# Linear attention and a gated feed-forward on one core: scores as pairs of 64-row tiles, weight loads as jobs of the order, two normalisations on GpSimd

## The chip, the core and the metric

The kernel runs on one core of a Trainium2 chip. A core has a matrix engine (TensorE, "PE" in the profile, its weight loads "PEld"), a vector engine (VectorE, "DVE"), a scalar engine (ScalarE, "ACT"), GpSimd ("POOL"), which computes and also issues the loads from memory, and SyncE ("SP"), which issues stores and transposing transfers. Each engine works through its own list of instructions in order and waits on semaphores for the others. Matrix results land in PSUM, eight banks of 128 partitions by 512 fp32. The metric is the device time of one launch in microseconds, as the median of several runs.

## What is computed

```python
k_proj = np.einsum('ks,bhsd->bhkd', E, k)          # 8 batches, 8 heads, 1024 x 64 -> 64 x 64
v_proj = np.einsum('ks,bhsd->bhkd', F, v)
scores = (1/8) * np.matmul(q, k_proj.transpose(0, 1, 3, 2))
scores = scores - np.max(scores, axis=-1, keepdims=True)
attn = np.exp(scores)
attn = attn / (np.sum(attn, axis=-1, keepdims=True) + 1e-09)
x = np.matmul(attn, v_proj)                        # -> (8192 tokens, 512)
gate = 1.0 / (1.0 + np.exp(-(x @ w_gate)))         # 512 -> 1536
val = x @ w_val
out = (gate * val) @ w_out                         # 1536 -> 512
```

All inputs are fp32; they are turned to bf16 on loading.

## The kernel before

Eight batches of 1024 tokens go through attention one after another, and each batch's tokens go through the feed-forward part as two blocks of 512. The feed-forward products are mostly made with seven instead of eight partial products (Winograd's form of Strassen's scheme): `quad_jobs` and `o_jobs` write them, with sums of weights (`w_sum`, `o_sum`), of inputs (`xs_sum`) and of hidden values (`s_sum`) made on VectorE and GpSimd. The first block is made plainly, by `plain_steps`.

A load puts eight consecutive tokens of a head on one partition, so a 128-column piece of Q holds two groups of tokens (g = 0, 1), 64 features each. After transposing, `qT[:, h, t * P : (t + 1) * P]` has on its 128 rows the 64 features of group 0 and the 64 of group 1, for token tile t (four tiles a batch) and head h. The projected keys stand in `kpD[:, h, :]` as a block diagonal: rows 0 to 63 and columns 0 to 63 for group 0, the rest for group 1, and zeros elsewhere. `score` (L1615) makes a score with one full 128x128 weight load and one matmul of 128 columns per head, four heads to a bank; half of what is multiplied is zero. So a token tile has two visits of TensorE (y = 0, 1), each into one bank. Behind it `highest` (L1633) takes the maximum on VectorE, `lower` (L1647) subtracts it (on VectorE for the later batches), `exps` (L1671) takes the exponential on ScalarE into `pt`, and `turn_p` sends the tile through a transposing transfer to `eT`.

Three kinds of TensorE jobs use a part of the array: the K and V projections (`project0`, `project_v0`, `kv`, `apart`: two tiles of 128 rows by 64 columns) and the first batch's output (`h_xo`: four tiles of 64 by 64, in two banks). All others use the full array.

The first batch has its own path in halves (`first_batch`, L784): projections as the halves of K and V land, scores, `total0` and `norm0` (sum, reciprocal, normalisation; L976, L983), transposes on TensorE, outputs. There `ORDER` also holds negative numbers, which `busy` (L720) turns into fillers: matmuls of the identity, -2 for 512 columns and -1 for 256, that keep TensorE going while it would wait.

Nothing is scheduled at run time. Each step is registered as a job in the order of the code; `ORDER` (L159) lists the job numbers in the order in which they are put on their engines, and `PLACES` (L314) lists the PSUM bank or SBUF buffer of each. The positions, costs and landing times (`AT`, `FB`, `K_AT`, `LAND`) given to `job` do nothing in this program: `Scheduler.job` drops them.

All loads go through GpSimd's queue. `start_loads` (L614) issues 25 of them ahead of every job: halves of K and Q, V, then the gate and value weights in column blocks j = 0 to 5, G (gate) and V (value), the first in halves (h0, h1).

Of the kernel before, what the change touches and what calls it, by code (L numbers as in the profile page):

```python
# [40 lines left out]
    f_pv00=0, f_pv01=0, f_pv10=1, f_pv11=1, f_s00=1, f_s01=1, f_s10=0, f_s11=0, f_n00=0, f_n01=0, f_n10=1,  # L41
# [3 lines left out]
    f_dk=0, f_w2=1, f_late=0, f_q1=0, f_q2=0, f_wsG0=1, f_wsG1=0, f_wsG2=0, f_wsV0=1, f_wsV1=0, f_wsV2=0,  # L45
    f_xs0=0, f_xs1=0, tx10=-22.239, tx11=-8.952, f_tx100=1, f_tx101=0, f_tx110=1, f_tx111=0, late0=-3.063,
# [107 lines left out]
class Job:  # L154
# [220 lines left out]
def bass_linformer_attn__then__ffn_glu_sigmoid_kernel(  # L375
# [20 lines left out]
    with contextlib.ExitStack() as es:  # L396
# [197 lines left out]
        def load_q_half(b, hf, R):  # L594
# [5 lines left out]
                f"Q{hf}{R}",  # L600
            )

        def load_w(j, ih=None):
            c = slice(256 * j, 256 * j + 256)
            ii = slice(0, NI) if ih is None else slice(2 * ih, 2 * ih + 2)
            for n in "GV":
# [7 lines left out]
        def start_loads():  # L614
# [18 lines left out]
            for R in range(2):  # L633
                load_q_half(0, 1, R)
# [1271 lines left out]
```

## Time and profile before

| what | value |
|---|---|
| time, median of 3 runs | 518.73 us (518.05 to 519.34) |
| the profiled execution | 517.88 us, of which 516.1 us is the span |
| granted clock of TensorE | 1.00 |
| VectorE, ScalarE, GpSimd busy | 85%, 73%, 33% |
| one score matmul, 128x128 by 128 columns | 219 ns from start to end, 56 ns from start to start in a row |
| maximum, subtraction, exponential of a 128x512 bank | 0.68, 0.69, 0.60 us |
| first normalisation, VectorE and GpSimd | 0.68 and 1.05 us |
| the first loads land (16th of 16 parts of a load) | K 6.5, 7.9, 10.6, 11.9; Q 9.2, 13.3; V 15.8, 17.1, 18.5 us |
| the weights land | 19.9 (G0h0), 20.3 (V0h0), 21.0 (G0h1), 21.7 (V0h1), 23.0 (G3), 24.4 (V3), 25.7 (G1), 27.1 (V1), 28.4 and 29.7 (second halves of Q), 31.1 (G4), 32.4 (V4), 34.2 (G2), 35.3 (V2), 36.6 (G5), 38.0 (V5) |

The span runs from the first to the last instruction; what lies around it is the launch. Matmuls are pipelined, so the distance between starts, not the duration of one, is what a matmul costs TensorE. In a timeline's line the first number is the start, the second the time until the last of the merged instructions ends, and x4 the number of instructions.

### The profile page before, as it was taken

Reading aid. Unit: us, or ns where it says so; the run is one execution under the profiler, and the core shown is the slowest. Engines: PE = TensorE matmul, PEld = TensorE weight load, DVE = VectorE, ACT = ScalarE, POOL = GpSimd, SP = SyncE. Lnnn points to the kernel's source line nnn. Section 1 sums busy time; section 2 is a strip of 40 time slices with the busy share of each in tenths; the row PEclk is TensorE's granted clock in tenths of the full one; section 3 lists DMA queues with packets and bytes.
Section 4 is the critical chain, followed back from the end, with each engine's and each line's share of the span. In section 5 each row is a group of like instructions: output and inputs, shape, how many; then the busy total and the mean of one; then the engine's idle time right before and its main releaser. Section 6 shows DMA issues by size and latency. Waiting matters only on the chain.

```text
span 516.1 us, 12124 instructions
## 1 busy us (share of the span) xinstructions
PE 509.8 (99%) x4716; PEld 424.0 (82%) x4719; DVE 437.7 (85%) x849; ACT 374.3 (73%) x714; POOL 169.8 (33%) x196
## 2 busy tenths in 40 slices
PE   8999999999999999999999999999999999999997
PEld 4455868889988899888998888888998889988884
DVE  7779998699987999969997799978989889968771
ACT  1666956888876796768967689777878679686652
POOL 9882004610535033340246113620052502403020
PEclk9999999999999999999999999999999999999999
DMA  9999948896679945994669837797565995430204
GB/s 168 197 198 207 187 63 173 135 206 124 144 143 174 189 91 128 169 175 103 122 147 170 156 104 130 157 180 127 142 99 113 197 193 100 98 89 1 83 2 163
DMA packets 140521, 71.57 MB, mean 139 GB/s; under 512 B 97200, under 2 KB 132272, under 8 KB 140464
## 3 DMA queue, kind: packets, MB, share of 16 engines
q0 software_dynamic: 35904, 29.89, 38.0%
q1 hardware_dynamic: 104560, 40.91, 37.8%
q8 instruction: 37, 0.61, 0.5%
q14 instruction: 20, 0.16, 0.1%
HBM read 60.29 MB, written 16.78 MB: 149 GB/s over the span
## 4 chain that ended last, share of the span: by engine, by line
PE 91%; DMA 3%; POOL 3%; DVE 1%; issue 0%; ACT 0%; POOLq 0%
PE pA L517 46%; PE pF L517 45%; DMA wG<-in_moe_w_gate_dram 3%; POOL KVs L558 1%; POOL wG L558 1%; POOL wV L558 1%; DVE hS L546 1%; POOL Qb L558 1%; DVE hT L1057 0%; DVE ost L1405 0%; DVE xT L877 0%; DVE hT L546 0%; ACT ost L531 0%; DVE tV L546 0%; DVE wV L546 0%
## 5 line engine op out<-in xcount | busy, mean ns | idle before, releaser
L531 ACT ACTIVATE spare<-pF 128x512 f32<-128x512 f32 (+2 forms) x167 | 94.3, 574 | 32.1 <-PE pF L517 22.6
L546 POOL TENSOR_TENSOR hT<-hT,hS 128x512 bf16<-128x512 bf16 x42 | 48.1, 1163 | 173.6 <-PE pA L517 98.6
L531 ACT ACTIVATE spare<-pA 128x512 f32<-128x512 f32 (+2 forms) x146 | 83.7, 586 | 20.3 <-PE pA L517 16.4
L1725 POOL TENSOR_TENSOR KVs<-spare,inv 128x384 bf16<-128x384 f32 (+1 forms) x41 | 29.6, 731 | 84.4 <-DVE topf L1636 35.3
L531 ACT ACTIVATE spare<-spare 128x512 f32<-128x512 f32 x74 | 46.2, 628 | 5.9 <-DVE spare L1147 5.5
L1147 DVE TENSOR_TENSOR spare<-pF,spare 128x512 f32<-128x512 f32 x59 | 40.1, 682 | 9.7 <-PE pF L517 4.8
L1216 DVE SCALAR_TENSOR_TENSOR hT<-spare,pF 128x512 bf16<-128x512 f32 x60 | 40.8, 680 | 7.7 <-PE pF L517 3.7
L517 PE MATMUL pA<-wO,hT 128*128 128x256 bf16 (+1 forms) x336 | 47.2, 280 | 0.0
L1147 DVE TENSOR_TENSOR spare<-pA,spare 128x512 f32<-128x512 f32 x54 | 36.7, 682 | 8.5 <-PE pA L517 6.4
L1216 DVE SCALAR_TENSOR_TENSOR hT<-spare,pA 128x512 bf16<-128x512 f32 x52 | 35.3, 680 | 8.3 <-PE pF L517 4.1
L517 PE MATMUL pF<-wO,hT 128*128 128x256 bf16 (+1 forms) x273 | 41.6, 295 | 0.2
L517 PE MATMUL pF<-xT,wV 128*128 128x256 bf16 (+1 forms) x248 | 39.9, 283 | 0.0
L517 PEld LDWEIGHTS pA<-wO,hT 128*128 128x128 bf16 x336 | 32.8, 98 | 6.6 <-ACT KVs L531 0.2
L517 PE MATMUL pA<-xS,wV 128*128 128x256 bf16 x248 | 37.2, 273 | 0.0
L517 PE MATMUL pA<-xT,wG 128*128 128x256 bf16 (+1 forms) x220 | 35.5, 284 | 0.7 <-DVE xT L877 0.5
L517 PE MATMUL pF<-xS,wG 128*128 128x256 bf16 x232 | 34.1, 272 | 0.0
L517 PEld LDWEIGHTS pF<-wO,hT 128*128 128x128 bf16 x276 | 26.6, 98 | 8.7
L517 PE MATMUL pF<-xS,tV 128*128 128x256 bf16 x224 | 33.6, 273 | 0.0
L517 PE MATMUL pA<-xS,tG 128*128 128x256 bf16 x208 | 31.2, 273 | 0.0
L517 PE MATMUL pF<-xT,wG 128*128 128x256 bf16 (+1 forms) x188 | 30.9, 286 | 0.0
L531 ACT ACTIVATE EF<-pA 128x512 f32<-128x512 f32 (+2 forms) x35 | 19.7, 564 | 14.2 <-PE pA L517 13.3
L517 PEld LDWEIGHTS pF<-xT,wV 128*128 128x128 bf16 x248 | 23.9, 98 | 4.3
(186 smaller groups left out, 1286.3 us busy)
## 6 DMA issues: line engine op xcount, KB each, us to landing
out_dram<-ost SPq DMA_DIRECT2D x63, 256.0 KB, 2.4
KVs<-in_v_dram POOLq DMA_DIRECT2D x15, 512.0 KB, 9.5
KVs<-in_k_dram POOLq DMA_DIRECT2D x14, 512.0 KB, 10.4
Qb<-in_q_dram POOLq DMA_DIRECT2D x14, 512.0 KB, 8.8
wO<-in_moe_w_out_dram POOLq DMA_DIRECT2D x1, 1536.0 KB, 27.9
wG<-in_moe_w_gate_dram POOLq DMA_DIRECT2D x5, 256.0 KB, 15.8
wV<-in_moe_w_val_dram POOLq DMA_DIRECT2D x5, 256.0 KB, 16.4
KVs<-in_k_dram POOLq DMA_DIRECT2D x4, 256.0 KB, 6.3
```

What stands on the lines that cost most here:

```text
L517: lambda e: e.matmul(o, lhsT, rhs, **kw),
L531: lambda e: e.activation(o, i, func, scale=scale),
L546: fn = lambda e: e.tensor_tensor(o, a, b, op)
L558: add("POOL", lambda e: e.dma_start(o, i), r=r, w=w, dma=sem, cost=0.78, nbytes=nbytes)
L1147: lambda e: e.tensor_tensor(PB(b)[:, :] if stay else BF(s), PB(b)[:, :], BF(s), ALU.add),
L1216: lambda e: e.scalar_tensor_tensor(o, y.rearrange("p (j c) -> p j c", j=2), 1.0, x.rearrange("p (j c) -> p j c", j=2), ALU.add, ALU.mult,),
L1725: fn = lambda e: e.tensor_tensor(xto.rearrange("p (g h d) -> p h g d", g=2, h=H)[:, hh[0] : hh[1], :, :], o[:, :, 0:DH].rearrange("p (h g) ...
```

## The change

Four things change, and with them all of `ORDER` and `PLACES`.

**Scores of batches 1 to 7.** `score_pair` takes the place of `score` (the first batch keeps `score`). A head's score is now two matmuls: the upper 64 rows with the upper left block of `kpD`, the lower 64 with the lower right one, each with 64 columns, at tile positions (0, 0) and (64, 0), into two banks by group. A token tile is one visit instead of two, with 16 weight loads and 16 matmuls instead of 8 and 8. Each bank now holds one group of all eight heads; `exps` therefore writes pieces of 64 columns, every second one, into `pt`.

**Loads.** The weight loads behind the first pair, and the second halves of Q, are jobs (`later_loads`), so `ORDER` puts them among GpSimd's other work. w3 comes in halves as w0 did, and the first block's steps of w3 are cut in two like those of w0.

**First normalisations.** Of the eight, the two of the first two token tiles and heads 0 to 3 go from VectorE to GpSimd (`f_n000`, `f_n001`).

**Dead code.** A path that `f_late=0` left unused is taken out.

```diff
-        def load_w(j, ih=None):
+        def load_w(j, ih=None, ns="GV"):
...
             load_w(0, 0)
-            load_w(0, 1)
-            load_w(3)
-            load_w(1)
+
+        def later_loads():
+            def one(f):
+                job("POOL", 0.0, f, name="loadw")
+
+            for j, ih in ((3, 0), (0, 1), (3, 1), (1, None)):
+                for n in "GV":
+                    one(lambda j=j, ih=ih, n=n: load_w(j, ih, n))
             for R in range(2):
-                load_q_half(0, 1, R)
-            load_w(4)
-            load_w(2)
-            load_w(5)
+                one(lambda R=R: load_q_half(0, 1, R))
+            for j in (4, 2, 5):
+                for n in "GV":
+                    one(lambda j=j, n=n: load_w(j, None, n))
...
-                eng = "POOL" if FB[f"f_n{hf}{R}"] > 0 else "DVE"
+                eng = "POOL" if FB[f"f_n{hf}{R}" if hf else f"f_n0{R}{t}"] > 0 else "DVE"
...
-                cut = (0, 2, 4) if m < 2 else (0, 4)
+                cut = (0, 2, 4) if m // 2 in (0, 3) else (0, 4)
...
-        def exps(b, t, y, bk):
-            o, r, w = pt[:, t, 512 * y : 512 * y + 512], [("projected", 0)], [("pt", t, y)]
-            act(o, PB(bk)[:, :], r, w, b=bk, func=AF.Exp)
+        def score_pair(t, bks):
+            for h in range(H):
+                for g in range(2):
+                    gg = slice(64 * g, 64 * g + 64)
+                    mm(
+                        bks[g],
+                        PB(bks[g])[:, 64 * h : 64 * h + 64],
+                        qT[gg, h, t * P : (t + 1) * P],
+                        kpD[gg, h, gg],
+                        [("kpD", h // 4), ("qT", h // 2), ("qTh", t // 2, h // 4, h % 4 // 2)],
+                        start=h == 0,
+                        stop=h == H - 1,
+                        read=True,
+                        tp=(64 * g, 0),
+                        n=64,
+                        conc=2,
+                        fill=0.0,
+                    )
+
+        def exps(b, t, g, bk):
+            o = pt[:, t, :].rearrange("p (h g k) -> p g h k", g=2, k=64)[:, g, :, :]
+            i = PB(bk)[:, :].rearrange("p (h k) -> p h k", k=64)
+            act(o, i, [("projected", 0)], [("pt", t, g)], b=bk, func=AF.Exp)
...
         def score_jobs(b, pos, step, late):
             for t in range(4):
-                for y in range(2):
-                    score_job(b, t, y, pos + step * (2 * t + y), late)
+                new_group()
+                bks = [new_bank(), new_bank()]
+                job("PE", pos + step * 2 * t, lambda t=t, bks=bks: score_pair(t, bks), name="sc")
+                for g in range(2):
+                    p = pos + step * (2 * t + g) + late
+                    bk = bks[g]
+                    job("DVE", p, lambda t=t, g=g, bk=bk: highest(b, t, g, bk), name="top")
+                    eng = "PE" if by_pe(b, t, g) else "DVE"
+                    job(eng, p + AT["pesub" if eng == "PE" else "dsub"], lambda t=t, g=g, bk=bk: lower(b, t, g, bk), name="sub")
+                    job("ACT", p + AT["dexp"], lambda t=t, g=g, bk=bk: exps(b, t, g, bk), name="exp")
```

The new `ORDER` is too long to print. Read with the job numbers that the code gives, it says:

| what | before | after |
|---|---|---|
| fillers of 512 and of 256 columns, all ahead of the first feed-forward matmul | 13 and 4 | 24 and 4 |
| score visits of batches 1 to 7 on TensorE, token tiles in each | single full-array visits, no mode change | batch 1: 3, 1; 2: 1, 2, 1; 3: 2, 2; 4: 2, 2; 5: 2, 2; 6: 1, 2, 1; 7: 1, 1, 2 (17 visits) |
| second batch's V projection | in one visit with the first batch's last output | alone, behind the first score visit |
| GpSimd's queue behind V0h0 | G0h1, V0h1, G3, V3, G1, V1, the two halves of Q, G4, V4, G2, V2, G5, V5; then V of batch 1, w_out, the sums of w0 and w3 | G3h0, V3h0, G3h1, V0h1, a half of Q, G0h1, V3h1, normalisation, G1, normalisation, a half of Q, G4, V4, V1, G2, G5, V2, V5, seven sums of w0 and w3, w_out; K and V of batch 1 behind the second half's normalisations |

More of the change, by code (lines that the diff above doesn't have):

```diff
@@ L40 @@
     ms=-2.738, xs0=1.022, ld1=24.087, lda=-2.888, f_pk00=1, f_pk01=1, f_pk10=1, f_pk11=0, f_tk0=1, f_tk1=0,
-    f_pv00=0, f_pv01=0, f_pv10=1, f_pv11=1, f_s00=1, f_s01=1, f_s10=0, f_s11=0, f_n00=0, f_n01=0, f_n10=1,
+    f_pv00=0, f_pv01=0, f_pv10=1, f_pv11=1, f_s00=1, f_s01=1, f_s10=0, f_s11=0, f_n000=1, f_n001=1, f_n010=0, f_n011=0, f_n10=1,
     f_n11=1, f_tq000=1, f_tq001=1, f_tq010=0, f_tq011=1, f_tq100=1, f_tq101=0, f_tq110=0, f_tq111=0,
@@ L44 @@
     f_xo001=0, f_xo010=0, f_xo011=1, f_xo100=0, f_xo101=0, f_xo110=0, f_xo111=1, f_dp=0, f_dx=1, f_dq=1,
-    f_dk=0, f_w2=1, f_late=0, f_q1=0, f_q2=0, f_wsG0=1, f_wsG1=0, f_wsG2=0, f_wsV0=1, f_wsV1=0, f_wsV2=0,
-    f_xs0=0, f_xs1=0, tx10=-22.239, tx11=-8.952, f_tx100=1, f_tx101=0, f_tx110=1, f_tx111=0, late0=-3.063,
+    f_dk=0, f_w2=1, f_q1=0, f_q2=0, f_wsG0=1, f_wsG1=0, f_wsG2=0, f_wsV0=1, f_wsV1=0, f_wsV2=0,
+    f_xs0=0, f_xs1=0, tx10=-22.239, tx11=-8.952, f_tx100=1, f_tx101=0, f_tx110=1, f_tx111=0,
     f_ou100=0, f_ou101=1, f_ou102=1, f_ou103=1, f_ou110=0, f_ou111=0, f_ou112=1, f_ou113=0,
@@ L428, in bass_linformer_attn__then__ffn_glu_sigmoid_kernel @@
         pt0 = within([P, 2, 1024], BF16)
-        xt0 = within([P, 2, 1024], BF16)
         quad = sbuf("quad", [P, 1], FP32)
@@ L601, in load_q_half @@
             )
-        def load_w(j, ih=None):
+        def load_w(j, ih=None, ns="GV"):
             c = slice(256 * j, 256 * j + 256)
             ii = slice(0, NI) if ih is None else slice(2 * ih, 2 * ih + 2)
-            for n in "GV":
+            for n in ns:
                 load(
@@ L756, in bass_linformer_attn__then__ffn_glu_sigmoid_kernel @@
         job = sched.job
+        later_loads()
         def h_xo(hf, R, bks):
@@ L784, in first_batch @@
         def first_batch():
-            K_AT, Q_AT = ((6.4, 8.05), (10.65, 12.0)), ((9.35, 13.4), (28.8, 30.1))
-            V_AT = ((15.9, 15.9), (18.35, 19.45))
+            K_AT, Q_AT = ((7.05, 8.4), (11.1, 12.45)), ((9.8, 13.75), (29.1, 30.45))
+            V_AT = ((16.35, 16.35), (17.7, 19.05))
             ENGS = ("ACT", "DVE", "POOL")
@@ L803, in tile @@
                 bk = new_bank()
-                sb = None if hf and FB["f_late"] else new_buf()
+                sb = new_buf()
                 p = FB[f"sc{hf}{R}"] + 0.003 * (t % 2)
@@ L808, in tile @@
                 job("PE" if by_pe(0, t, R) else "DVE", p, lambda: lower(0, t, R, bk), name="sub")
-                if hf and FB["f_late"]:
-                    job("ACT", p, lambda: exp_late(t, R, bk), name="exp")
-                    return
                 job("ACT", p, lambda: exp0(bk, sb), name="exp")
                 job("DVE", p + FB["dsum"], lambda: total0(t, R, sb), name="psum")
-                eng = "POOL" if FB[f"f_n{hf}{R}"] > 0 else "DVE"
+                eng = "POOL" if FB[f"f_n{hf}{R}" if hf else f"f_n0{R}{t}"] > 0 else "DVE"
                 job(eng, p + FB["dnorm"], lambda: norm0(t, R, sb, eng), name="norm")
@@ L841, in first_batch @@
                         job("SP", FB["tp11"], lambda t=t: send_p0(t), name="turnp")
-                if hf and FB["f_late"]:
-                    for R in range(2):
-                        for t in (2, 3):
-                            for x in range(2):
-                                h = 4 * R + 2 * x
-                                n = 2 * (t % 2) + x
-                                p = FB[f"xo1{R}"] + 0.003 * n
-                                out_job(0, t, (h, h + 2), p, FB["late0"], FB[f"f_ou1{R}{n}"] > 0)
-                        for t in (2, 3):
-                            if not FB["f_dx"]:
-                                step(
-                                    "tx", f"1{R}", t % 2,
-                                    lambda b, t=t, R=R: turn_x0(t, R, b),
-                                    [lambda b, eng, t=t, R=R: turned_x0(t, R, b, eng)],
-                                )
-                    for t in (2, 3):
-                        if FB["f_dx"]:
-                            job("SP", FB["tx11"], lambda t=t: send_x0(t), name="turnx")
-                    continue
                 for R in range(2):
@@ L944, in exp0 @@
             act(BF(s), PB(bk)[:, :], [], [bf_(s)], b=bk, func=AF.Exp)
-        def exp_late(t, R, bk):
-            act(pt0[:, t % 2, 512 * R : 512 * R + 512], PB(bk)[:, :], [], [("pt0", t % 2, R)], b=bk, func=AF.Exp)
-        def turn_x0(t, R, b):
-            def src(x):
-                g, i = x // 2, 2 * R + x % 2
-                c = 512 * g + 128 * i
-                return xt0[:, t % 2, c : c + 128]
-            turns(b, src, [("xt0", t % 2, 2 * x) for x in (2 * R, 2 * R + 1)])
-        def turned_x0(t, R, b, eng):
-            hf, c = t // 2, P * (t % 2)
-            i = PB(b)[:, :].bitcast(BF16)[:, 0:512].rearrange("p (g i c) -> p g i c", g=2, i=2)
-            copy(eng, xT[0][:, hf, :, 2 * R : 2 * R + 2, c : c + P], i, [], [("xTt", 0, t, R)], b, 512)
-        def send_x0(t):
-            hf, c = t // 2, P * (t % 2)
-            add(
-                "SP",
-                lambda e: e.dma_start_transpose(
-                    xT[0][:, hf, :, :, c : c + P].rearrange("p g i c -> p (g i) c"), xt0[:, t % 2, :]
-                ),
-                r=[("xt0", t % 2, x) for x in (0, 2, 4, 6)],
-                w=[("xTt", 0, t, R) for R in range(2)],
-                dma=f"xT{t}",
-                cost=1.26,
-                nbytes=256 << 10,
-            )
         def total0(t, R, s):
@@ L1012, in bass_linformer_attn__then__ffn_glu_sigmoid_kernel @@
         LAND = {
-            "G": (20.1, 21.45, 26.1, 34.2, 23.5, 31.5, 36.85),
-            "V": (20.75, 22.15, 27.5, 35.5, 24.8, 32.9, 38.25),
+            "G": (19.7, 22.6, 26.4, 34.65, 23.95, 32.1, 37.3),
+            "V": (20.4, 23.3, 27.8, 36.0, 25.05, 33.35, 38.7),
         }
+        EARLY = {"G": (19.7, 21.1), "V": (20.4, 22.0)}
         def landed(n, j):
@@ L1040, in plain_steps @@
                 pos = FB[f"m{m // 2}"] + FB["ms"] * (m % 2)
-                cut = (0, 2, 4) if m < 2 else (0, 4)
+                cut = (0, 2, 4) if m // 2 in (0, 3) else (0, 4)
                 for a, b in zip(cut, cut[1:]):
                     for n, bb, dp in (("G", bg, 0.0), ("V", bv, 0.1)):
-                        rel = landed(n, m // 2) if m // 2 or a else LAND[n][0]
+                        rel = landed(n, m // 2) if m // 2 not in (0, 3) or a else EARLY[n][m // 6]
                         job(
@@ L1248, in o_sum @@
             w = [("wT", n)] + [("pt0", x, y) for x in range(2) for y in range(2)]
-            w += [("xt0", x, y) for x in range(2) for y in (0, 2, 4, 6)]
             dve(lambda e: e.tensor_tensor(T[n], a, b, op), r, w, n=1536, rate=1.92)
@@ L1723, in divide @@
             i = inv[:, n0 : n0 + 2 * k]
-            xto = xt[:, t, :] if b else xt0[:, t % 2, :]
+            xto = xt[:, t, :]
             fn = lambda e: e.tensor_tensor(
@@ L1730, in divide @@
             )
-            r = [("inv", t, h) for h in range(*hh)] + ([("projected", 1)] if b else [])
-            w = [("xt", t, hh[0]) if b else ("xt0", t % 2, hh[0])]
+            r = [("inv", t, h) for h in range(*hh)] + [("projected", 1)]
+            w = [("xt", t, hh[0])]
             if s is None:
@@ L1750, in turn_x @@
             )
-        def score_job(b, t, y, p, late):
-            new_group()
-            bk = new_bank()
-            job("PE", p, lambda: score(t, y, bk), name="sc")
-            job("DVE", p + late, lambda: highest(b, t, y, bk), name="top")
-            eng = "PE" if by_pe(b, t, y) else "DVE"
-            job(eng, p + late + AT["pesub" if eng == "PE" else "dsub"] * (b > 0), lambda: lower(b, t, y, bk), name="sub")
-            job("ACT", p + late + AT["dexp"] * (b > 0), lambda: exps(b, t, y, bk), name="exp")
         def score_jobs(b, pos, step, late):
             for t in range(4):
-                for y in range(2):
-                    score_job(b, t, y, pos + step * (2 * t + y), late)
+                new_group()
[8 more added lines that the diff above has]
+                    job("ACT", p + AT["dexp"], lambda t=t, g=g, bk=bk: exps(b, t, g, bk), name="exp")
                 job("SP", pos + step * (2 * t + 1) + AT["dturn"], lambda t=t: turn_p(t), name="turnp")
```

358 rows, old and new, of tables (ORDER, PLACES) are left out of this document.

## The prediction, made before the changed kernel was run

> **What bounds the kernel now.** I read the page first: the busy line, the slices, the chain of waits.
>
> ```profile
> span 516.1 us, 12124 instructions
> PE 509.8 (99%) x4716; PEld 424.0 (82%) x4719; DVE 437.7 (85%) x849; ACT 374.3 (73%) x714; POOL 169.8 (33%) x196
> PE   8999999999999999999999999999999999999997
> PEclk9999999999999999999999999999999999999999
> ```
>
> TensorE is busy in every slice at full clock, and 91% of the chain that ended last is TensorE. A busy TensorE may still stand still between modelled ends, so I took the starts of the matmuls one by one and compared each distance with what the same shape takes in a row (256 columns 109 ns, 512 columns 216 ns, 128 columns 56 ns). From 62 us on some 1.8 us in all is left over, apart from the mode changes below. So after 62 us a nanosecond of TensorE's stream is a nanosecond of the kernel. Next the timeline of TensorE around one of today's score tiles:
>
> ```profile
> 177.88 0.60 PE L517 MATMUL pF<-xT,wV 128*128 128x256 bf16 x4
> 178.31 0.39 PE L517 MATMUL pF<-kpD,qT 128*128 128x128 bf16 x4
> 178.54 0.60 PE L517 MATMUL pF<-xS,wG 128*128 128x256 bf16 x4
> ```
>
> Start to start, four score matmuls take 178.31 to 178.54, 56 ns each, and nothing is lost on either side. Now the same timeline where TensorE leaves the full 128 by 128 array and comes back, at a K/V projection (two column tiles) and at the first batch's output (four 64 by 64 tiles):
>
> ```profile
> 110.95 0.60 PE L517 MATMUL pF<-xT,wV 128*128 128x256 bf16 x4
> 111.48 1.92 PE L517 MATMUL pF<-KVs,EFT 128*64 128x512 bf16 x16
> 113.33 0.50 PE L517 MATMUL pA<-xS,tG 128*128 128x256 bf16 x3
> ...
> 43.16 0.59 PE L517 MATMUL pF<-xT,wV 128*128 128x512 bf16 x2
> 43.69 0.41 PE L517 MATMUL pF<-eT,vpD 64*64 64x256 bf16 x8
> 44.03 0.40 PE L517 MATMUL pA<-ident,wT 128*128 128x128 bf16 x4
> ```
>
> Four matmuls of 109 from 110.95 end at 111.39, but the projection starts at 111.48: 0.09 us lost. Its 8 pairs of 216 ns would take 1.73 and take 1.85: 0.12 more. With 0.01 at the next matmul a visit to a tiled mode costs 0.22. The second visit: 0.10 on the way in, 0.345 for two groups of 109 (0.13 too many), 0.01 behind: 0.24. Inside a visit the tiles do run side by side: the groups of four take 109 ns, not 436, though they write two banks.
>
> Last, the timeline of the first 22 us, where TensorE waits for loads and copies, and fillers (ident x ident) stand in the holes:
>
> ```profile
> 10.62 0.63 PE L517 MATMUL pA<-KVs,EFT 128*64 128x256 bf16 x8 [0.19 <-DMA KVs<-in_k_dram]
> 14.53 1.14 PE L517 MATMUL pA<-ident 128*128 128x512 bf16 x5
> 19.97 0.41 PE L517 MATMUL pF<-eT,vpD 64*64 64x256 bf16 x8 [0.29 <-ACT eT L531]
> 21.70 0.59 PE L517 MATMUL pF<-xT,wV 128*128 128x512 bf16 x2
> ```
>
> The last line is the first matmul of the feed-forward part. From there on TensorE loses only 0.19 (24.1 us), 0.20 (30.2), 0.36 (34.3) and 0.70 (48.6) up to 62 us.
>
> **The change part by part**, against the profiled span of 516.1 us (517.9 with what lies around it, 0.8 under the median of 518.73; I take the difference over to the median).
>
> Scores, streaming. Seven batches have 28 token tiles; each has 8 full matmuls of 56 ns today: 224 x 56 = 12.5 us. Each becomes 8 pairs of 64 rows by 64 columns. No row has this shape. Lower bound of a pair: the rows give 109 for 256, 56 for 128, so some 2.5 ns plus 1/2.4 ns a column, 29 ns for 64. Upper bound: 56, if the tiles ran one behind the other or weight loads, now twice as many, set the pace. For the loads the single records help: behind an idle stretch the second 128-column load follows the first by 15 ns, the second 64-column load in a narrow tile by 28, and loads of different tiles start 3 to 4 ns apart. A pair's two loads should thus take 15 ns side by side under a 29 ns pair. I take 29, nearest to the 64 by 64 rows where tiles overlap: 224 x 29 = 6.5, a gain of **6.0** (0 to 6.0).
>
> Visits. The 28 tiles stand in the new order in 17 visits (7 of one tile, 9 of two, 1 of three), none next to another tiled job; 17 x 0.22 = 3.75, and one projection that shared a visit with an output of the first batch now has its own, 0.1: **+3.85** (3.4 at 0.20 to 4.3 at 0.24 with the split at 0.2).
>
> Readers of the scores. Maximum, subtraction and exponential stay 56 each of 128x512 (0.68, 0.69 and 0.60 us); the exponential writes pieces of 64, which on a 73% busy ScalarE I take at nothing (0 to 0.1 each, hidden). A visit of two fills four of the eight banks at once; see the rivals.
>
> First normalisations. DVE loses two of 0.68, GpSimd gains two of 1.05 (the rows of the other four). They stand in GpSimd's queue behind seven and eight of the weight loads, and the later loads wait behind them. Issues are 0.73 us apart, so the last load is issued near 23 instead of 19.9 us. The landings in the trace follow one another by 1.34 us per 512 KB to 38.0 us, 8 to 19 us behind their issues: 3 us are covered. The first gate half (w3) lands in the second half's old place, 21.0. The sums of weights follow on GpSimd, and w_out moves behind seven of them, from 22.7 to some 32 us; the queue still has loads to 38, so this is hidden as well; the second batch's K and V loads come at 45 to 49 and land by some 56 (K) and 61 (V), just ahead of their projections. If that cover went, each late load would cost up to 2.5 us, its own time.
>
> Start. Eleven more fillers of 0.216 (24 against 13) are 2.4 us of stream. From 7.19 us, TensorE's work up to the first feed-forward matmul is: seven half-projections of 0.66 and a shared visit of 1.0 (5.6), 18 short groups of about 0.22 (4.0), fillers 5.6: 15.2, so 22.4 at the earliest. Walking the new order with today's durations of copies, maxima and exponentials I find 0.2 more of waits: 22.6 against 21.70, **+0.9** (-0.6 when landing alone decides, 21.05; +1.5).
>
> 22 to 62 us. Arriving 0.9 later TensorE meets the loads landed: the holes of 0.19 and 0.36 go; the other two I leave: **-0.55** (-1.45 to 0). Behind 62 us: 0 (-1 to +3.4, rival two).
>
> Sum: -6.0 + 3.85 + 0.9 - 0.55 = -1.8. Span 514.3, median **516.9**.
>
> A rule against this. In this trace the next load of the same 128 rows starts 2 ns behind the start of the matmul before it, and the score matmuls still keep 56 ns. The Trainium skill, TensorE: Matmul & The Clock Gate, "The mechanism", says that a weight load overlaps a running matmul only when their row groups differ; for full tiles the trace doesn't bear it out. By it a pair would be some 44 ns and the sum +1.5.
>
> **Rivals.**
>
> One, the weight loads set the pace (slower). Place: the pairs. If a load of a 64-row tile goes at the narrow tiles' rate, 128 columns take twice 27 = 54 ns, a pair is 56, the gain of 6.0 is gone: 522.9. If it waits for the matmul before it, 29 + 15 = 44: 520.2. It decides from 37 ns on, where 224 x 19 = 4.2 only pays visits and start. For it: narrow tiles do load slower in the rows. Against: they have 64 columns, these have 128. The Trainium skill, TensorEngine Tiling (Array Packing), "Gotcha 2: Feature Incompatibilities", takes fast weight load from column tiling only; no run here shows it for rows. Two tiles that don't run side by side would come to the same 522.9; the groups of four speak against it.
>
> Two, visits wait for banks. Two tiles want four banks free together, while products hold three each and the vector engine (85% busy) has to read each score bank twice. If TensorE waited half a read (0.34) at ten visits, 3.4: 520.3. For: one wait of this size today, 0.65 at 211 us, behind a sum of the vector engine. Against: 1.8 us of waits of all kinds in 450.
>
> Three, the start is worse: a normalisation on GpSimd delays its transposes by more than the walk shows, another 1.5 at 22 us: 518.4.
>
> Four, better: the new order has none of the holes of the first 62 us (-1.45) and starts no later: some 515.0.
>
> **How the numbers follow.** The forecast 0.50 (its own range 515.6 to 518.2), rival one 0.16, two 0.17, three 0.07, four 0.10. About 0.3%, 1.6 us, is what a measurement can tell from no change: bounds 517.2 and 520.3. Faster: 0.37 of the forecast's 0.50 and all of four: 0.47. Same: 0.13 + 0.03 + 0.08 + 0.06 = 0.30. Slower: 0.13 of one, 0.09 of two, 0.01 of three: 0.23. The range reaches from 515.2, most of case four, to 521.0, which takes in rival two and rival one at 44 ns.
>
> **What would show it.** Pairs of 64x64 matmuls 29 ns apart from pair to pair; 17 stretches with about 0.2 us lost around each; the first feed-forward matmul near 22.6; no new named waits of TensorE behind 62 us. A pair distance above 37 ns, bank waits at the visits of two, or GpSimd's loads landing later than 39 us would make the forecast wrong.

## The result and the profile after

The changed kernel takes 520.13 us (median of 15 runs, 519.43 to 523.33); beside it the kernel before took 518.40 (518.00 to 519.80). The ratio is 1.0037, with a 95% interval of 1.0025 to 1.0050: slower by 1.7 us, where 1.8 us faster was forecast. The profiled execution took 520.55 us, with a span of 518.7.

The page of the changed kernel, for the same lines as before the change:

```profile
span 518.7 us, 12593 instructions
PE 510.6 (98%) x4954; PEld 418.9 (81%) x4954; DVE 434.2 (84%) x847; ACT 373.0 (72%) x714; POOL 171.5 (33%) x200
PE   8999999989999999999999999999999999999997
```

The span is 2.6 us longer with TensorE busy for 0.8 us more: the rest is TensorE standing still, and the ninth slice (104 to 117 us) now shows an 8. The timeline of TensorE in the changed kernel, at the first feed-forward matmul, at a visit of two score tiles, and at three of its longest stops:

```profile
22.54 0.59 PE L516 MATMUL pA<-xT,wG 128*128 128x512 bf16 x2
...
183.03 0.82 PE L516 MATMUL pA<-wO,hT 128*128 128x256 bf16 x6
183.79 0.41 PE L516 MATMUL pF<-kpD,qT 64*128 64x64 bf16 x16
184.03 0.40 PE L516 MATMUL pA<-kpD,qT 64*128 64x64 bf16 x16
184.36 0.72 PE L516 MATMUL pA<-wO,hT 128*128 128x256 bf16 x5
...
115.52 1.99 PE L516 MATMUL pA<-KVs,EFT 128*64 128x512 bf16 x16 [1.42 <-DMA KVs<-in_k_dram]
253.77 0.34 PE L516 MATMUL pF<-vpD,eT 128*128 128x130 bf16 x3 [0.47 <-ACT KVs L530]
377.10 0.29 PE L516 MATMUL pF<-vpD,eT 128*128 128x130 bf16 x2 [0.48 <-DMA eT<-KVs]
```

Six matmuls of 109 ns from 183.035 end at 183.69, and the visit starts at 183.79; its 16 pairs would take 0.46 and take 0.57. The visit costs 0.10 + 0.11 and 0.01 behind, some 0.21 (forecast 0.22). The first feed-forward matmul stands at 22.54, forecast 22.6. The single records of a visit show the pairs:

```profile
424.61 0.19 PE L516 MATMUL pA<-kpD,qT 64*128 64x64 bf16 x1
424.62 0.19 PE L516 MATMUL pF<-kpD,qT 64*128 64x64 bf16 x1
424.64 0.19 PE L516 MATMUL pA<-kpD,qT 64*128 64x64 bf16 x1
424.64 0.19 PE L516 MATMUL pF<-kpD,qT 64*128 64x64 bf16 x1
424.67 0.19 PE L516 MATMUL pA<-kpD,qT 64*128 64x64 bf16 x1
```

From one pA to the next it is 0.03 us, 29 ns to the nanosecond of the trace (38 to 40 from the first pair of a visit to its second, which the price of the visit holds). What is new is in the view of waits, TensorE alone, from 62 us on (us in total, times, longest):

```profile
PE pA L516 <- DMA KVs<-in_k_dram: 1.4, 1, 1.4
PE pF L516 <- DMA eT<-KVs: 0.5, 1, 0.5
PE pF L516 <- ACT KVs L530: 0.5, 1, 0.5
PE pF L516 <- issue: 0.4, 1, 0.4
PE pA L516 <- DMA kpD<-kpd: 0.3, 1, 0.3
```

The kernel before has one such line there, 0.5 us behind a sum of VectorE. Three of these five name transfers, and the one put down to "issue", at 88.78 us, follows a transposing transfer that landed at 88.69. The longest is at the projection of the third batch (batch 2): the first half of its K lands last of six loads, at 115.47. In the old order that half was the fourth; in the new one two halves of Q go ahead of it, and each load takes some 3.2 us of the transfers' full throughput.

**Three terms tell every execution apart.** I summed what TensorE loses between the starts of its matmuls from 62 us on, above the distance of each shape, without the mode changes and without the few matmuls that the trace lacks. The span less this sum, less the start of the first feed-forward matmul, leaves the work of TensorE behind the start. (By this sum the kernel before has 1.31, where the prediction had some 1.8.) All of it but the time is from one profiled execution of each kernel (us):

| kernel | time | span | first feed-forward matmul | waits behind 62 us | rest |
|---|---|---|---|---|---|
| before | 518.4 to 518.8 | 516.1 | 21.70 | 1.31 | 493.1 |
| changed | 520.13 | 518.7 | 22.54 | 6.06 | 490.1 |
| r1_k2_first | 518.76 | 517.0 | 23.13 | 3.78 | 490.1 |
| r2_slack | 518.15 | 516.5 | 23.02 | 3.46 | 490.0 |
| r3_full_array | 521.23 | 519.4 | 22.67 | 4.02 | 492.7 |
| r4_fewer_fillers | 519.19 | 517.3 | 22.79 | 4.28 | 490.2 |
| r5_moved | 518.17 | 516.5 | 23.18 | 3.37 | 490.0 |
| r6_moved_full | 519.93 | 518.2 | 22.84 | 2.66 | 492.7 |
| r7_one_tile | 520.54 | 518.8 | 23.24 | 3.75 | 491.8 |
| r8_norms_dve | 520.50 | 518.3 | 23.11 | 5.04 | 490.2 |
| r9_moved_again | 518.25 | 516.6 | 23.12 | 3.60 | 489.9 |
| r10_before_moved | 518.24 | 516.8 | 22.30 | 1.59 | 492.9 |
| r11_tile_order | 519.08 | 517.3 | 22.73 | 4.52 | 490.1 |
| r12_no_hold | 516.61 | 514.8 | 23.02 | 2.02 | 489.8 |

The change takes 3.0 us out of the rest and adds 0.8 to the start, but 4.75 to the late waits. These two executions lie 2.7 us apart and the medians 1.7, so some 0.9 of the 4.75 may belong to these two executions alone. The stops behind the four transfers (at 88.8, 115.5, 377.1 and 424.5 us) make 3.2 of the 6.06, the one at 253.8 another 0.6, and the remainder comes in pieces of some 0.2 and less. The experiments ask whether these waits are owed to places in the new order, or whether the scores themselves cost what shows as waits.

### The profile page after: what moved, and what is told of

Same layout as the page of the kernel before. It is cut to its first block, busy times and chain, and to the rows that moved or that the text cites. A ratio compares the mean times of both kernels' runs of the same rounds, so it can differ in the third digit from the quotient of the medians.

```text
span 518.7 us, 12593 instructions
## 1 busy us (share of the span) xinstructions
PE 510.6 (98%) x4954; PEld 418.9 (81%) x4954; DVE 434.2 (84%) x847; ACT 373.0 (72%) x714; POOL 171.5 (33%) x200
## 4 chain that ended last, share of the span: by engine, by line
PE 92%; DMA 4%; POOL 1%; DVE 1%; ACT 0%; issue 0%; POOLq 0%; ACTq 0%
PE pF L516 50%; PE pA L516 43%; DMA KVs<-in_k_dram 3%; DMA eT<-KVs 1%; POOL hT L545 1%; DVE topf L1590 1%; DMA kpD<-kpd 1%; DVE pF L1617 0%; ACT KVs L530 0%; POOL xS L545 0%; POOL KVs L557 0%; POOL Qb L557 0%; ACT EFT L530 0%; DVE pA L1617 0%; ACT ost L530 0%
## 5 line engine op out<-in xcount | busy, mean ns | idle before, releaser
L1699 POOL TENSOR_TENSOR KVs<-spare,inv 128x384 bf16<-128x384 f32 (+1 forms) x50 | 35.9, 730 | 106.2 <-PE pA L516 31.9
L516 PE MATMUL pF<-wO,hT 128*128 128x256 bf16 (+1 forms) x408 | 60.3, 291 | 0.0
L516 PEld LDWEIGHTS pF<-wO,hT 128*128 128x128 bf16 x408 | 39.3, 98 | 11.8 <-issue 0.4
L516 PE MATMUL pA<-xT,wV 128*128 128x256 bf16 (+1 forms) x208 | 34.4, 287 | 0.0
L516 PE MATMUL pF<-xT,wV 128*128 128x256 bf16 (+1 forms) x200 | 32.4, 283 | 0.0
L516 PE MATMUL pA<-xS,wV 128*128 128x256 bf16 x200 | 29.7, 273 | 0.0
L516 PE MATMUL pF<-wT,hT 128*128 128x256 bf16 x216 | 28.3, 273 | 0.0
L516 PE MATMUL pA<-wO,hT 128*128 128x256 bf16 (+1 forms) x204 | 27.2, 279 | 0.0
L516 PE MATMUL pF<-wT,hS 128*128 128x256 bf16 x204 | 27.2, 273 | 0.0
L516 PE MATMUL pA<-xS,wG 128*128 128x256 bf16 x184 | 27.1, 272 | 0.0
```

The lines of the kernel that those rows point to most:

```text
L516: lambda e: e.matmul(o, lhsT, rhs, **kw),
L1699: fn = lambda e: e.tensor_tensor(xto.rearrange("p (g h d) -> p h g d", g=2, h=H)[:, hh[0] : hh[1], :, :], o[:, :, 0:DH].rearrange("p (h g) ...
```

## The experiments

**One load, r1_k2_first.** In the order of GpSimd's jobs the load of the first half of Q (job 419) goes behind that of K (415):

```diff
-    ... 472, 570, 521, 419, 460, 462, 535, ... 490, 479, 537, 415, 423, 491, 542, ...
+    ... 472, 570, 521, 460, 462, 535, ... 490, 479, 537, 415, 419, 423, 491, 542, ...
```

> The changed kernel with one load moved: the third batch's second half of Q goes behind its second half of K in GpSimd's order, everything else the same. Theory A (the pairs gain what was forecast, and the new order gives it back in some seven places where TensorE arrives ahead of a transfer or a read): the wait of 1.5 us at 115.5 us goes, 520.1 - 1.4 = 518.7. Rival B (the change of the scores itself costs, and waits only show where the surplus comes out): the time stays at 520.1 and another wait of about that size appears behind.

Measured: 518.76 us, ratio 1.0004 (0.9995 to 1.0012). One load by one place gives 1.4 of the 1.7 us back, as theory A has it. (By the code it is the halves of heads 0 to 3 that change places, the first and not the second ones.) The projection starts without a wait ahead of it:

```profile
114.52 1.70 PE L522 MATMUL pA<-KVs,EFT 128*64 128x512 bf16 x14
```

**Slack where it is late, r2_slack.** The move of r1, two Q loads of the fifth batch behind its K, and seven moves of TensorE's jobs, so that what needs a late transfer or bank comes a few jobs later (at 88.8, 253.8, 327.4, 377.1 and 424.5 us). Two of them, by the names of the jobs (Q: a feed-forward product, xo: an output of attention, sc: scores of a token tile, O: a product with w_out):

```diff
-  Q22G2S2, xo4.t0x0, Q22G1A12
+  Q22G2S2, Q22G1A12, xo4.t0x0
-  Q39G6S4, sc7.t1, Q41V0A11
+  Q39G6S4, Q41V0A11, sc7.t1
```

> The changed kernel with the loads of two batches put K and V ahead of Q, and five jobs of TensorE that arrive at a landing or at an exponential too early put behind one to three neighbours that are ready (sums of the named waits 1.5 + 0.6 + 0.6 + 0.6 + 0.4 + 0.1 = 3.9 us). No instruction is added or taken away. Theory A: 516.2, faster than both kernels. Rival B: above 519.

Measured: 518.15 us, ratio 0.9989 (0.9981 to 0.9998): 2.0 of the hoped 3.9. Its waits of TensorE from 62 us on:

```profile
PE pF L522 <- ACT pF L536: 0.2, 1, 0.2
PE pA L522 <- ACT KVs L536: 0.2, 1, 0.2
PE pF L522 <- issue: 0.2, 1, 0.2
```

No transfer is left among them. But 3.46 us of waits remain, in pieces of 0.4 and less behind ScalarE and VectorE: where TensorE comes earlier it meets the copies that free a bank. The time lies between the two theories, so the next runs had to price the scores with the waits small.

**Full-array scores, r3_full_array and r6_moved_full.** The pairs become matmuls of all 128 rows, with the zeros of `kpD` in them; banks, readers and order stay. r3 has the order of the changed kernel, r6 that of r5_moved below:

```diff
-                        qT[gg, h, t * P : (t + 1) * P],
-                        kpD[gg, h, gg],
+                        qT[:, h, t * P : (t + 1) * P],
+                        kpD[:, h, gg],
...
-                        tp=(64 * g, 0),
                         n=64,
-                        conc=2,
-                        fill=0.0,
```

> The changed kernel with its order and banks, but each pair as two matmuls of the full array (128 rows, the block diagonal's zeros included, 64 columns), so without tile modes. Stream: 28 x 16 x 29 = 13.0 us instead of 6.5; no visits, 17 x 0.21 = 3.5 less. Theory A: +3.0, 523.1, or down to 521.6 where the slower stream fills waits. Rival B (pairs and their mode changes cost as much as they save or more): 520 or below.

Measured: 521.23 us, only 1.1 above the changed kernel. Its timeline at the visit of 183.79:

```profile
184.57 0.63 PE L516 MATMUL pF<-kpD,qT 128*128 128x64 bf16 x16
185.03 0.63 PE L516 MATMUL pA<-kpD,qT 128*128 128x64 bf16 x16
185.50 0.71 PE L516 MATMUL pA<-wO,hT 128*128 128x256 bf16 x5
```

Two tiles take 0.93 us without loss at the edges, against 0.57 + 0.11. By the table the rest grows by 2.6, near the expected 2.9, and the late waits shrink by 2.0: the slower scores fill them. So my number missed (1.1 more, where 1.5 to 3.0 was expected), while the work moved as theory A has it; that the slower stream fills the waits is read from this sum alone, and TensorE's signals come less late here too (see r11_tile_order).

> The order of the run with 43 more moves, with the score pairs as full-array matmuls of 128 rows and 64 columns. Theory A: 224 times 29 ns more (6.5 us) less 17 visits of 0.21 us (3.6 us), with few waits left that a slower stream could fill: 2.3 to 2.9 us more than the same order with pairs. Rival B (pairs are worth nothing net): within 1 us of it.

Measured: 519.93 us, 1.76 above r5_moved, under the band. The rest is again 2.7 up, waits 0.7 and the start 0.3 down. With the visits paid, the pairs are worth 2.7 us of TensorE's work against these matmuls, and less in time as long as waits lie behind them.

**Visits, r7_one_tile.** A feed-forward job goes between the token tiles of a visit, for instance

```diff
-  O4.0A11j0, sc3.t0, sc3.t1, O4.0A11j1
+  O4.0A11j0, sc3.t0, O4.0A11j1, sc3.t1
```

> The order of the run with 43 more moves, with all but one of the visits of two or three token tiles split by a feed-forward job put between the tiles: 27 visits in place of 17. Theory A: ten more visits of 0.21 us, 1.7 to 2.1 us more than the same order unsplit. Rival: entering and leaving the 64-row tiles is hidden beside the stream of matmuls or the waits, then within 0.4 us of it.

Measured: 520.54 us, 2.4 above r5_moved and over the band: 1.8 in the rest (0.18 for each of ten visits, expected 0.21) and 0.4 in waits. In its trace a visit still costs 0.21 each, but one of the new ones stands next to a K projection and costs 0.11. Visits are not hidden; packing two tiles to a visit was worth doing.

**Fillers, r4_fewer_fillers.** 11 of the 24 fillers of 512 columns are left out, which compute nothing that is used.

> The changed kernel with 13 instead of 24 fillers of 512 columns in the first 22 us, spread as in the kernel before. If the fillers stand on TensorE's path, the first feed-forward matmul comes at 21.1 to 21.8 instead of 22.5 us, and the time falls by what the landings behind don't take back: 519.1 to 519.7. If the chain of copies and exponentials ends last there anyway, it stays at 22.5 and 520.1.

Measured: 519.19 us, as if fillers lay on the path, but the profile says no. The start of its feed-forward part:

```profile
22.02 0.38 PE L522 MATMUL pF<-ident,wT 128*128 128x128 bf16 x4 [0.27 <-ACT xT L536]
...
22.79 0.59 PE L522 MATMUL pA<-xT,wG 128*128 128x512 bf16 x2
```

The first feed-forward matmul is not earlier (22.79 against 22.54, where 21.1 to 21.8 was expected): waits take the fillers' place. The gain is 1.8 us of late waits; the stops at 88.8, 377.1 and 424.5 are missing in this execution. At 377 the transposing transfer took 3.12 us from issue to landing here and 4.90 in the changed kernel. Why it is sooner here stays open.

**First normalisations, r8_norms_dve.** `f_n000` and `f_n001` are set back to 0, nothing else.

> The changed kernel with the two first normalisations back on VectorE, all else as changed. As predicted (hidden): the changed kernel's 520.1 within 0.5. Rival (GpSimd's slower normalisations, or the weight loads queued behind them, are on the path of the start): 519.2 or less, with the first feed-forward matmul ahead of 22.3 us.

Measured: 520.50 us, inside the band of "hidden"; the first feed-forward matmul stands at 23.11. The two normalisations on GpSimd show no cost.

**Order of tiles in a visit, r11_tile_order.** In the changed kernel VectorE's first read of a score bank, where VectorE is free, starts some 0.31 us behind the recorded end of the last matmul into that bank, and 0.62 at two visits; with full-array scores in the same order (r3) it is some 0.11 and 0.19. The two visits had the tile that is read first in second place:

```diff
-    ... 1323, 1333, 1494, 1492, 1324, 1325, 1484, ...
+    ... 1323, 1494, 1492, 1324, 1325, 1333, 1484, ...
```

> The changed kernel with the two token tiles exchanged within two visits, the second of the fifth batch and the first of the sixth, so that the tile that VectorE reads first comes first. If the reader waits for the last matmul of a visit to leave the 64-row tiles: its first read follows its tile's last pair by some 0.3 us in place of 0.63, and TensorE's wait of 0.63 us for ScalarE at 253.8 us shrinks to 0.3. If the read's delay has another cause, both stay. The time, 520 us, can't tell it.

The read at the second visit of the fifth batch, in the changed kernel

```profile
250.76 0.69 DVE L1590 TENSOR_REDUCE topf<-pF 128x8 f32<-128x512 f32 x1 [0.56 <-PE pF L516]
```

and with the tiles exchanged

```profile
250.16 0.69 DVE L1596 TENSOR_REDUCE topf<-pF 128x8 f32<-128x512 f32 x1
```

The bank's last matmul ended by its record at 250.14 and 249.86: 0.62 became 0.30 us, and TensorE's stop of 0.63 us at 253.8 is gone. Its single execution took 519.08 us. Reading a score bank later is a cost that the forecast had at nothing; of the long stops it made this one.

The expectation had leaving the 64-row tiles as a possible cause. The records of TensorE's semaphore, on whose steps the other engines wait, show another: in none of the 14 traces do two of these signals stand less than 34 ns apart, and here nearly every score matmul gives one (392 of 448), because the program lets the writes of the next batch's keys and queries wait for each of them. The two matmuls of a pair come every 29 ns, so the signals fall behind: by 32 x 34 - 16 x 29 = 624 ns at the end of a visit of two tiles, by half of that behind one. With full-array matmuls, one in 29 ns, it is 32 x 5 = 160 ns. In the last batch, which no later one follows, a visit gives only one signal per bank, and there the same read comes 0.04 and 0.07 us behind at the two visits where VectorE is free. Of the signals behind 62 us, 328 come over 0.15 us behind their matmul in the changed kernel and none in the kernel before; 42 of these belong to other jobs behind a visit. What they add to the smaller waits no run shows, nor what a kernel with one signal per bank would take.

**Moves by the profile, r5_moved, r9_moved_again.** Both are orders with single jobs moved where the profile of the run ahead showed TensorE waiting (43 moves, then 21 more). One of the 21:

```diff
-  Q22G1A12, xo4.t0x0, Q23V5A22, xo4.t0x1, O6.5A22j0
+  Q22G1A12, xo4.t0x0, Q23V5A22, O6.5A22j0, xo4.t0x1
```

> The changed kernel with the moves of the earlier run that gave TensorE slack at eight places, and 43 more moves of single jobs in the order: jobs of TensorE that waited there for a bank or a transfer go behind the next ones, and some readers on ScalarE and VectorE come earlier. Scores, visits, loads and amount of work stay. Theory A (the pairs gain what was forecast, and late waits give it back): with the profile of that earlier run showing 1.7 us of waits over 115 ns and 1.7 us of smaller ones behind 62 us, some 2 us of them go: 516.0 to 517.0 us, below the kernel before and near the forecast of 516.9. Rival B (the score change itself costs, or waits only move to the next place): 517.8 to 518.5.

Measured: 518.17 us (ratio 0.9986, 0.9977 to 0.9995), as r2_slack: the waits went from 3.46 to 3.37 only.

> The order of the run with 43 more moves, with 21 further moves at the waits that its own profile still shows (behind 62 us 1.9 us of waits over 115 ns, 1.5 us of smaller ones), the reads of scores now counted 0.25 us later behind a visit, as its trace has them. Theory A (late waits took back the gain and can be removed): 517.0 to 517.6 us, half of the 1.5 us that a walk through the orders gives. Rival B (waits only move from place to place): 517.9 to 518.5, as before these moves.

Measured: 518.25 us (0.9989, 0.9981 to 0.9998). Rival B had these two right: what was removed came out elsewhere. But its profile now holds most of the waits in one stop. VectorE's, GpSimd's and TensorE's timelines of r9_moved_again around it:

```profile
221.33 4.36 DVE L1177 SCALAR_TENSOR_TENSOR hT<-spare 128x512 bf16<-128x512 f32 x1
...
221.73 3.40 POOL L551 TENSOR_TENSOR hT<-hT,hS 128x512 bf16<-128x512 bf16 x3
...
226.98 0.61 PE L522 MATMUL pF<-xT,tV 128*128 128x256 bf16 x4 [1.50 <-ACT spare L536]
```

A product of VectorE that takes 0.68 us at most other places takes 4.36. It ends 0.56 us behind the third of GpSimd's sums; ScalarE's copy and TensorE come after it. In r5_moved the same product took 2.40 us beside the same three sums. Moving TensorE's jobs couldn't cure this.

**A control, r10_before_moved.** 26 such moves on the kernel before.

> A control: the kernel before, scores and loads as they were, with 26 moves of single jobs found in the same way at its own waits (0.8 us over 115 ns and 0.5 us of smaller ones behind 62 us, 1.7 us between 22 and 62). Theory A (what the moves gain on the changed kernel is owed to its own late waits): little is to be had here, 517.6 to 518.5 us. Rival C (any order gains as much by such moves, so the moved orders say nothing on the change): 516.5 to 517.2.

Measured: 518.24 us (0.9991, 0.9982 to 0.9999), inside the band of A. It says less than hoped: its late waits didn't shrink (1.59 against 1.31), so what a better order could give the kernel before stays open. Its held sum at 209.7 us (2.09 us, see the last section) was left in place.

**Without the held product, r12_no_hold.** Three jobs of VectorE come earlier than in r9_moved_again; TensorE, ScalarE, GpSimd and the transfers keep their order:

```diff
 xS<-xS,xT (1176)
+hT<-hT (1279)
+hT<-hT (1280)
 spare<-pA,spare x2 (ending with 1268)
-hT<-hT (1279)
-hT<-hT (1280)
 hT<-spare (1269)
```

> The order with 43 and 21 moves, and three more on VectorE alone: two sums and the product of the hidden values of pass 20 come a few instructions earlier, so that this product no longer begins beside three sums of GpSimd at 221.7 to 225.1 us. In the profile of the order without these three moves that product (hT<-spare, its operands in SBUF) lasted 4.36 us in place of 0.68, ended 0.56 us behind GpSimd's last sum, and TensorE then waited 1.67 us at 227.0, the longest wait of that kernel. If VectorE is held there by GpSimd: the product takes 0.7 us, that wait goes, and the time falls by 1.2 to 1.7 us from 518.25, to 516.5 to 517.0. If the wait has another cause, or what is removed comes out at the next place: 517.8 to 518.4.

Measured: 516.61 us (516.16 to 516.76), ratio 0.9957 (0.9943 to 0.9971): 2.0 us below the kernel before and 3.5 below the changed one, with the scores, the visits and the work of the change. The product, GpSimd's sums and the page of this kernel:

```profile
220.39 0.69 DVE L1177 SCALAR_TENSOR_TENSOR hT<-spare 128x512 bf16<-128x512 f32 x1
...
222.33 3.42 POOL L551 TENSOR_TENSOR hT<-hT,hS 128x512 bf16<-128x512 bf16 x3
...
224.48 0.68 DVE L1177 SCALAR_TENSOR_TENSOR hT<-EF,pF 128x512 bf16<-128x512 f32 x1
```

```profile
span 514.8 us, 12590 instructions
PE 510.2 (99%) x4954; PEld 419.0 (81%) x4954; DVE 433.9 (84%) x847; ACT 372.5 (72%) x714; POOL 172.0 (33%) x200
```

The product takes 0.69 us, and the view of waits names none of TensorE from 62 us on (those over 0.15 us; by the table 2.02 us are left in smaller ones). The forecast had a span of 514.3 and 516.9 us for a change without new late waits. This kernel comes within 0.5 and 0.3 us of that, but after 77 moves of single jobs, and with a later start (+1.3) and more waits (+0.7) than the kernel before, against 3.3 less of the rest. No run gave the kernel before as many moves.

## Why the prediction was wrong

**Score streaming, -6.0: right.** 29 ns a pair, 224 pairs in 6.5 us. Rival one, weight loads setting the pace at 44 or 56 ns, fell: behind the first pair of a visit they stand 29 or 30 ns apart, but for two stops of 0.1 us and less. In these rows the loads of the next pair start 2 ns behind the matmuls of the pair before. The Trainium skill, TensorE: Matmul & The Clock Gate, "The mechanism", would have such a load wait for a matmul of the same rows; the trace doesn't agree.

**Visits, +3.85: right**, 17 times 0.21 and the split projection; 0.18 each when ten were added.

**Start, +0.9: right in size, with luck.** 22.54 against 21.70, but in the profiles with the same start (all but r4, r8 and the two of the kernel before) it lies between 22.54 and 23.24, so the changed kernel's is the earliest of ten; r10, with the start of the kernel before, has 22.30. The eleven fillers weren't what set it, as the sum had it: with them gone it was no earlier. Rival three, a worse start, holds some 0.7 us at most.

**22 to 62 us, -0.55: too careful.** From 1.45 us of stops 0.1 is left at 30.5 us, and 0.2 is new, in the second batch's K projection at 57.6 us: the second half of K landed at 57.73, where the working had some 56. That makes -1.1, near the end of the range.

As measured these four make -6.0 + 3.8 + 0.8 - 1.1 = -2.5, and the table shows -3.0 + 0.8 = -2.2. Up to here the time falls as forecast; 0.3 us isn't placed.

**"Behind 62 us: 0 (-1 to +3.4, rival two)" failed.** It was 4.75. Rival two had the size in reach but for the most part the wrong cause: it let visits wait for banks, and one stop of 0.63 us, at 253.8, was of that kind, from the late read of a score bank, and one of 0.1 between the two tiles of the visit at 310.8. The other long stops were transfers, 3.2 us together: the longest, 1.5 us, because two halves of Q had been put ahead of K in GpSimd's queue; putting one of them back was worth 1.4 us of the time (r1_k2_first). The working followed each load of the start and of the second batch by issue and landing, and stopped there; the loads of the later batches and the transposing transfers of SyncE were never held against TensorE's new times, and the signals of twice as many matmuls were not counted. In the changed kernel 26 transfers behind 60 us land less than 1.2 us ahead of the first instruction that reads them, against 6 before, and five of these start within 0.1 us of the landing. That is exposure and not yet a wait: r12_no_hold has 30 of them.

What isn't settled is how much of the 4.75 the change had to bring. r12_no_hold has the same work and 2.02 of waits, so most of it belonged to the places of jobs. But two rounds of moves only shifted waits until the held product was found. In the changed kernel that product isn't held; the moves brought it beside GpSimd's sums (1.09, 2.40, then 4.36 us). Others like it already stood in the kernel before.

## What to carry to other kernels

When work is taken off an engine that is busy 99% of the time, everything behind it is asked for earlier: go through each transfer and reader on the whole span, not the first stage alone, and compare its landing with the new time at which it is needed; a slack of under a microsecond can be a wait: one transposing transfer took 4.90 us in the changed kernel's execution and 3.12 in r4's. Count also how many short matmuls signal. Split a measured time into start, late waits and the rest before blaming the edit: here the rest moved as forecast while the time moved the other way. And when moving jobs of the stalled engine only shifts a wait, look for the instruction upstream that is longer than its own row says.

## What the hardware showed unexpectedly

**GpSimd holds VectorE.** A product of VectorE with both operands in SBUF takes 0.68 us, and 4.36, 2.40 and 1.09 us beside GpSimd's sums in r9_moved_again, r5_moved and r2_slack, each ending 0.55 to 0.56 us behind the last sum. A product of the same kind with one operand in PSUM isn't held: 224.48 above took 0.68 us while GpSimd's sums ran from 222.33 to 225.75. In the changed kernel 101 sums and products with an operand in PSUM begin inside a computation of GpSimd, and none takes over 2% longer for it; of those with all operands in SBUF three do, and all three are held. The kernel before has it too, a sum of VectorE beside GpSimd, and there it makes TensorE's longest late stop, 0.65 us at 211.4:

```profile
209.37 1.99 DVE L546 TENSOR_TENSOR hS<-hS,hT 128x1024 bf16<-128x1024 bf16 x1
...
209.64 1.17 POOL L546 TENSOR_TENSOR xS<-xT,xS 128x512 bf16<-128x512 bf16 x1
...
211.42 0.83 PE L517 MATMUL pF<-wT,hS 128*128 128x256 bf16 x6 [0.48 <-DVE hS L546]
```

The Trainium skill, SBUF — State Buffer, "Who interferes with whom", has a VectorE instruction with two inputs in SBUF contend with a GpSimd instruction that reads SBUF, over a pair of ports that is locked for one of them. The traces agree that only sums and products with all inputs in SBUF are held; but where the page lets the order of issue decide who waits, the product of 221.33 began by its record 0.4 us ahead of the first sum and was held through three of them.

**Signals of short matmuls queue.** TensorE's signals stand 34 ns apart at the least. Behind pairs that end every 29 ns VectorE's first read of a score bank came 0.31 us late, and 0.62 where the tile read is the last of two, against 0.11 and 0.19 with full-array matmuls in the same order, and 0.04 and 0.07 in the last batch, where most matmuls give no signal.

**Transposing transfers are slow beside loads.** Of the 90 in the changed kernel, 71 are issued while no load of GpSimd's runs: they land after 3.1 us in the median, at most 5.3. The 19 issued beside a load take 8.8 in the median and up to 14.4. In the kernel before only 10 were issued beside one.
